# Attention with decay and a softplus MLP: an early load of lam, other PSUM banks for chunk 0's state sums, and a new order of the opening steps

## The chip, the cores and the metric

The kernel runs on one core of one Trainium2 chip. The metric is the device time of one execution in microseconds (us), the median of several runs. An engine works through its own instruction stream in order and waits on semaphores for the others: TensorE (PE) multiplies, VectorE (DVE) and ScalarE (ACT) do elementwise work, SyncE (SP) issues most loads, and GpSimd (POOL) fills a few constants at the start.

## The reference

Two layers follow each other. The first is linear attention with a decay `lam` for each head, computed block by block with a running state; its output, 3072 tokens of 512 features, is the input `x` of an MLP with a softplus between two matrix products.

```python
for b in range(nb):                      # 12 blocks of 64 positions
    intra = einsum(q, k) * Dmask         # Dmask = lam ** (i - j) for i >= j
    intra = einsum(intra, v)
    inter = einsum(q * lam_pow, kv_state)
    out[:, :, sl] = intra + inter
    kv_state = lam_block * kv_state + einsum(k * rev_pow, v)
h = x @ w_in                             # 512 -> 2048
g = log1p(exp(-|h|)) + max(h, 0)         # softplus
return g @ w_out                         # 2048 -> 512
```

## The kernel before

The sequence is cut into 6 chunks of 128 positions, and the 8 heads into 4 pairs; a chunk and a pair make a unit, so that units 0 to 3 are chunk 0 and unit 4 is the first of chunk 1. The batch of 4 lies inside a unit. In chunk 0 the state is zero, so the first products are whole 128 x 128 score blocks (`scores0`, step S), masked on DVE (`mask0_scores`, m), multiplied with v (`out0`, O) and copied out as a high and a low half (`x0_high` on ACT, xh, and `x0_low` on DVE, xl). The state that chunk 1 starts from is the product of the decayed k with v (`k0_decay` or `k0_decay_act`, then `sums0`, Q), which ACT copies out of PSUM (`states0`, sc).

The MLP has 16 slices of d_ff for each chunk, 96 "slots" in all: slot s multiplies x with a slice of `w_in` (`mlp1`, step mlp; 12 products of 128 x 512), ACT and DVE make the softplus and its high and low halves (act, ghi, glo), and `mlp2` multiplies them with a slice of `w_out` (12 products). Each operand is a high and a low half, so every product is taken three times. The weights come as 64-bit floats and are converted on the chip once, in 32 half-megabyte pieces: scale and round and the high half (hi) on ACT; shift, sign, add and the low half (lo) on DVE. Piece numbers stand behind the step names: `lo 8 9` is the low half of pieces 8 and 9, and `mlp 0 2` is slot 0 with pair 2. Piece 8 is needed by `mlp2` of slot 2.

The order of the work is written out by hand. A string of some 170 steps is carried out first, in one order for all engines: each step appends its instructions to the streams of the engines it uses. Then a loop over slots 6 to 99 follows. Loads are steps as well (qk, v, kt for a unit's parts, load n for weight pieces up to n, unit n for whole units) and go to SP's queue; before the first scores a short second string gives the first loads. `warm n` issues n products on zeros, whose result is not used.

The eight PSUM banks form three pools: four "o" banks (`obank`: the zero products, chunk 0's scores, slots 2 and 3, then the four output sums of `mlp2`), one "t" buffer of two banks (`work`: z of chunk 0, the state sums y0, then scores and outputs of the later units, one after the other), and two "h" banks for the other slots' `mlp1`. A tile takes a buffer of its pool when an earlier tile there has been read for the last time.

Constants come from `lam_b`, lam spread over 128 partitions: a copy and a scan on DVE give the mask of chunk 0 (`mask0`), a copy on ACT and a second scan on DVE the powers `lp`.

Of the kernel before, what the change touches and what calls it, by code (L numbers as in the profile page):

```python
# [14 lines left out]
B, H, S, D = 4, 8, 768, 64  # L15
# [11 lines left out]
def half(i):  # L27
    return slice(i * 64, (i + 1) * 64)
# [3 lines left out]
def decay_attention_softplus_ffn(  # L32
# [7 lines left out]
    nc = tc.nc  # L40
# [7 lines left out]
    def t8(shape, dt, name):  # L48
        return sb.tile(shape, dt, tag="b8", bufs=21, name=name)
# [10 lines left out]
    def th(shape, dt, name):  # L60
        return sb.tile(shape, dt, tag="bh", bufs=5, name=name)

    def obank(name):
        return ps.tile([128, 512], F32, tag="o", bufs=4, name=name)

    def work(name):

        return ps.tile([128, 2, 512], F32, tag="t", bufs=1, name=name)
# [4 lines left out]


    lam_b = cp.tile([128, H], F32, name="lam_b")

    def load_lam():
        nc.scalar.dma_start(out=lam_b, in_=lam.rearrange("(o h) -> o h", o=1).broadcast_to([128, H]))

    units, raws = {}, {}  # L80

# [5 lines left out]
    def load_half(g, major):  # L87
        nc.sync.dma_start(out=unit(g)[:, major], in_=att[g // NP, g % NP, :, major])
# [18 lines left out]
    def kt_of(g):  # L107
        return part(g, 1, 0)

    def vt_of(g):  # L110
        return part(g, 1, 1)
# [10 lines left out]
    def w_load(n):  # L122
# [9 lines left out]
            n_raw += 1  # L132

    load_half(0, 0)
    load_lam()
    loads = {
        "qk": lambda g: load_half(g, 0), "v": lambda g: load_part(g, 1), "kt": lambda g: load_part(g, 0),
        "w": w_load, "unit": load_upto,
    }
    for line in "w 1".split(","):  # L140
        name, number = line.split()
        loads[name](int(number))

# [2 lines left out]
    warm = t8([128, 512], F32R, "warm")  # L146
# [3 lines left out]
    def keep_warm(n):  # L150
        for _ in range(n):
            nc.tensor.matmul(warm_ps, lhsT=warm[:, :128], rhs=warm, start=True, stop=True)

    keep_warm(18)

    mask0, step0 = (spare[:, 2 * n : 2 * n + 2].rearrange("q n (h i) -> q (n h) i", i=C) for n in range(2))
    begin0 = begin[:, 0:2].rearrange("q n (h i) -> q (n h) i", i=C)
# [16 lines left out]
        out=begin0, in_=ramp.rearrange("q (o i) -> q o i", o=1).broadcast_to([128, H, C]), scalar=0.0,  # L174
# [81 lines left out]
    lo, hi = half(0), half(1)  # L256
# [149 lines left out]
    x0, z, y = {}, {}, {}  # L406
# [42 lines left out]

    def sums0(*pairs):  # L450
        for p in pairs:
            if not y:
                y[0] = work("y0")
            kd, v = kt_of(p), vt_of(p)
            for b in range(B):
                for t in range(2):
                    c = (p % 2) * 256 + b * D
                    nc.tensor.matmul(
                        y[0][half(t), p // 2, c : c + D], lhsT=kd[:, b, t], rhs=v[:, b, t], start=True, stop=True
                    )  # L460

    def states0(p):
        st = states[p + NP] = th([128, B, 2, D], F32, f"st_{p + NP}")
        for t in range(2):
            c = (p % 2) * 256
            nc.scalar.copy(  # L466
                out=st[lo, :, t], in_=y[0][half(t), p // 2, c : c + 256].rearrange("q (b e) -> q b e", b=B)
            )

    def scores1(g):  # L470
# [3 lines left out]
    def out1(g):  # L474
# [3 lines left out]
    step = {  # L478
        "S": scores0, "m": mask0_scores, "O": out0, "xh": x0_high, "xl": x0_low, "kd": k0_decay, "kda": k0_decay_act,
        "Q": sums0, "sc": states0, "kd1": k_decay, "qd": q_decay, "sc1": scores1,  # L480
        "m1": lambda g: mask_scores(g, z[g][:, 0]), "up": lambda g: update_states(g, z[g][:, 1]), "out1": out1,
        "xh1": lambda g: x_high(g, z[g]), "xl1": lambda g: x_low(g, z[g]),
# [3 lines left out]
        "warm": keep_warm, "load": w_load, "unit": load_upto, "qk": loads["qk"], "v": loads["v"], "kt": loads["kt"],  # L486
    }
    for line in """
        round 0, qk 1, S 0, m 0 0, load 2, scale 0, m 0 1, shift 0, sign 0, scale 1, v 0, qk 2, warm 6, S 1,
        add 0, load 3, m 1 1, warm 2, O 0, m 1 0, hi 0, xh 0, shift 1, lo 0, sign 1, S 2, scale 2, xl 0, v  # L490
        1, qk 3, m 2 0, warm 2, mlp 0 0, v 2, load 4, m 2 1, O 1, round 2, round 1, shift 2, xh 1, kt 1, S
        3, add 1, sign 2, hi 1, scale 3, xl 1, kda 1, lo 1, O 2, mlp 0 1, round 3, xh 2, mlp 1 0, v 3, m 3
        1, load 5, m 3 0, mlp 1 1, add 2, kt 2, load 6, scale 4, shift 3, hi 2, xl 2, O 3, sign 3, lo 2, mlp
        0 2, kda 2, load 7, load 8, add 3, xh 3, kt 0, round 4, hi 3, unit 5, xl 3, shift 4, lo 3, mlp 1 2,
        scale 5, mlp 2 0, shift 5, mlp 0 3, scale 6 7, kt 3, sign 4, load 9, mlp 2 1, mlp 2 2, round 6 7,
        mlp 3 0, mlp 1 3, mlp 3 1, kda 0, shift 6 7, add 4, act 0, kd1 4, load 10, sign 6 7, ghi 0, sign 5,
        add 6 7, hi 4, hi 6 7, kd 3, glo 0, mlp 3 2, lo 6 7, load 11, lo 4, load 12, round 5, mlp 3 3, act
        1, mlp 2 3, Q 0, ghi 1, add 5, Q 1, scale 8 9, load 13, glo 1, hi 5, Q 2, shift 8 9, lo 5, Q 3, sc
        0, sign 8 9, act 2, load 14, sc 3, sc 1, sc 2, sc1 4, load 15, up 4, ghi 2, round 8 9, glo 2, act 3,
        mlp 5, m1 4, mlp 4, ghi 3, unit 6, unit 7, add 8 9, scale 10 11, hi 8 9, qd 4, mlp2 0, round 10 11,  # L500
        glo 3, act 4, shift 10 11, lo 8 9, sign 10 11, ghi 4, glo 4, add 10 11, load 16, mlp2 1
    """.replace("\n", " ").split(","):
        name, *numbers = line.split()
        step[name](*map(int, numbers))
# [7 lines left out]
    for s in range(6, last + LAG):  # L512
# [25 lines left out]
        if s in outs_at:  # L538
            g = outs_at[s]
            w = work(f"z{g}")  # L540
# [46 lines left out]
```

## Time and profile before

| what | value |
|---|---|
| median of 3 runs | 612.82 us (612.53 to 613.39) |
| the profiled execution | 613.22 us, its span 611.4 us |
| PE busy | 598.3 us, 98% of the span |
| DVE, ACT busy | 226.3 us, 211.2 us |
| moved by DMA | 48.95 MB, 20.00 MB of it in the first 60 us |

Times in the profile count from the start of the span. A row of the timeline shows start, length, engine, line and operation, output and input tiles, and a count; the bracket at its end is the idle time before it and what ended it. A row of the windows shows each engine's busy time and instructions in one stretch, then the granted TensorE clock, the DMA engines' busy share and the GB/s.

### The profile page before, as it was taken

To read this page: it belongs to the slowest core of one execution; us is meant where nothing else is said; L and a number is where in the kernel's file an instruction comes from. 1 tells how busy PE (TensorE), PEld (TensorE's weight loads), DVE (VectorE), ACT (ScalarE), POOL (GpSimd) and SP (SyncE) were. 2 spreads that over 40 slices of the span, in tenths; PEclk is the share of its full clock that TensorE was granted. 3 is DMA by queue.
4 is the path that set the end of the run, shared out by engine and by line. 5 is a ranking of instruction groups with operands and counts; after the bars stand their busy time and mean duration, and the time that the engine had idled before them with its cause. 6 is when DMAs were issued, how large, how long until landed. Compare 5 with 4: busy or idle time off the path is not lost.

```text
span 611.4 us, 11189 instructions
## 1 busy us (share of the span) xinstructions
PE 598.3 (98%) x5020; PEld 488.2 (80%) x5020; DVE 226.3 (37%) x337; ACT 211.2 (35%) x343; POOL 1.5 (0%) x9
## 2 busy tenths in 40 slices
PE   7969999999999999999999999999999999999997
PEld 5758888888888888888888888888888888888886
DVE  5978799833321232322313322222222121210111
ACT  3877677633222222321232232212322221322121
POOL 0000000000000000000000000000000000000000
PEclk9979999999999999999999999999999999999999
DMA  8994314205002024201020500210500100100001
GB/s 294 416 417 187 133 70 138 70 2 207 2 2 70 1 70 140 68 1 46 26 70 33 175 2 1 70 42 29 207 1 1 70 1 1 70 0 1 1 1 69
DMA packets 15743, 48.95 MB, mean 80 GB/s; under 512 B 1872, under 2 KB 1872, under 8 KB 15696
## 3 DMA queue, kind: packets, MB, share of 16 engines
q1 hardware_dynamic: 15264, 47.72, 21.3%
q8 instruction: 39, 0.64, 0.4%
q10 hardware_dynamic: 432, 0.53, 0.2%
q14 instruction: 8, 0.07, 0.0%
HBM read 41.95 MB, written 6.29 MB: 79 GB/s over the span
## 4 chain that ended last, share of the span: by engine, by line
PE 93%; DVE 3%; ACT 1%; issue 1%; DMA 1%; DVEq 0%
PE h L363 43%; PE o L380 43%; PE w L285 3%; PE z L298 2%; PE z L302 2%; DMA lam_b<-in_lam 1%; PE w L287 1%; DVE c L225 1%; DVE att L419 1%; ACT st L466 0%; DVE c L231 0%; ACT w L234 0%; PE z L429 0%; DVE c L221 0%; ACT l L344 0%
## 5 line engine op out<-in xcount | busy, mean ns | idle before, releaser
L363 PE MATMUL h<-x,w 128*128 128x512 f32 x1152 | 283.8, 396 | 0.4 <-DVE x L439 0.4
L380 PE MATMUL o<-w,g 128*128 128x512 f32 x1152 | 275.9, 389 | 0.0
L380 PEld LDWEIGHTS o<-w,g 128*128 128x128 f32 x1152 | 216.3, 188 | 44.8
L363 PEld LDWEIGHTS h<-x,w 128*128 128x128 f32 x1152 | 214.2, 189 | 47.1 <-DVE x L439 0.9
L352 DVE TENSOR_TENSOR g<-l,g 128x512 fp32r<-128x512 f32 x96 | 66.4, 691 | 264.6 <-ACT g L348 264.4
L344 ACT ACTIVATE l<-h 128x512 f32<-128x512 f32 x96 | 57.1, 595 | 269.7 <-PE h L363 261.5
L348 ACT CAST g<-l 128x512 fp32r<-128x512 f32 x96 | 59.6, 621 | 3.0
L269 ACT ACTIVATE kd<-att,rp 128x256 f32<-128x256 f32 x40 | 18.1, 501 | 59.9 <-DMA att<-in_att 59.9
L312 DVE SCALAR_TENSOR_TENSOR st<-st,lam_c,w 64x256 f32<-64x256 f32 x72 | 31.6, 479 | 4.3 <-PE w L287 3.5
L285 PEld LDWEIGHTS w<-att 64*64 64x64 f32 x640 | 21.1, 139 | 11.8 <-issue 6.0
L285 PE MATMUL w<-att 64*64 64x64 f32 x640 | 23.9, 226 | 5.0 <-ACT st L466 5.0
L335 DVE TENSOR_TENSOR x<-z,x 128x512 fp32r<-128x512 f32 x20 | 13.8, 691 | 35.2 <-ACT x L328 35.2
L274 DVE TENSOR_TENSOR qd<-att,lp 128x512 f32<-128x512 f32 x20 | 13.8, 689 | 34.1 <-DMA att<-in_att 34.1
L328 ACT CAST x<-z 128x512 fp32r<-128x512 f32 x20 | 11.7, 585 | 38.9 <-PE z L302 38.9
L287 PE MATMUL w<-att,kd 64*64 64x64 f32 x576 | 23.9, 227 | 0.0
L307 DVE TENSOR_TENSOR a<-w,mask 128x512 f32<-128x512 f32 x20 | 13.8, 690 | 25.7 <-PE w L287 19.5
L298 PEld LDWEIGHTS z<-qd,st 64*64 64x64 f32 x640 | 17.0, 134 | 7.0 <-issue 7.0
L287 PEld LDWEIGHTS w<-att,kd 64*64 64x64 f32 x576 | 21.1, 139 | 0.0
L298 PE MATMUL z<-qd,st 64*64 64x64 f32 x640 | 20.9, 224 | 0.0
L231 DVE CUSTOM_DVE_ANT_0 c<-raw,c 128x2048 uint16<-128x2048 uint16 (+1 forms) x19 | 20.0, 1054 | 1.4
L238 DVE TENSOR_TENSOR w<-c,w 128x1024 fp32r<-128x1024 f32 (+1 forms) x19 | 19.9, 1053 | 1.6 <-ACT w L234 1.3
L225 DVE SCALAR_TENSOR_TENSOR c<-raw,c 128x1024 uint32<-128x1024 uint32 (+1 forms) x19 | 19.9, 1054 | 0.4
(42 smaller groups left out, 183.2 us busy)
## 6 DMA issues: line engine op xcount, KB each, us to landing
att<-in_att SPq DMA_DIRECT2D x44, 512.0 KB, 4.8
raw<-in_wts SPq DMA_DIRECT2D x32, 512.0 KB, 8.7
out_dram<-ob SPq DMA_DIRECT2D x22, 256.0 KB, 2.4
att<-in_att SPq DMA_DIRECT2D x8, 256.0 KB, 7.8
out_dram<-ob ACTq DMA_DIRECT2D x2, 256.0 KB, 2.0
lam_b<-in_lam ACTq DMA_DIRECT2D x1, 4.0 KB, 6.4
```

Of the source, the lines that this page charges most:

```text
L225: nc.vector.scalar_tensor_tensor(out=c, in0=raw_at(ks, 1), scalar=0x80000000, in1=c, op0=ALU.bitwise_and, op1=ALU.bitwise_or)
L231: nc.vector.tensor_add(out=c, in0=c, in1=raw_at(ks, 0))
L238: nc.vector.tensor_sub(out=w[:, 1], in0=conv.pop(ks[0]).bitcast(F32), in1=w[:, 0])
L285: nc.tensor.matmul(x[r, cols], lhsT=k[r, b, t], rhs=q[r, b, t], start=True, stop=True)
L287: nc.tensor.matmul(y[half(1 - s), cols], lhsT=kd[r, b, t], rhs=v[r, b, t], start=True, stop=True)
L298: nc.tensor.matmul(w[half(t), s, cols], lhsT=st[r, b, t], rhs=qd[r, b, t], start=True, stop=False)
L312: nc.vector.scalar_tensor_tensor(out=to[:, :, t], in0=of[:, :, t], scalar=lam_c[r, h : h + 1], in1=u[:, :, t], op0=ALU.mult, op1=ALU.add,)
L344: nc.scalar.activation(l_tiles[s], h_tiles.pop(s), AF.Softplus)
L348: nc.scalar.copy(out=g_tiles[s][:, 0, :], in_=l_tiles[s])
L352: nc.vector.tensor_sub(out=g[:, 1, :], in0=l_tiles.pop(s), in1=g[:, 0, :])
L363: nc.tensor.matmul(h_tiles[s], lhsT=w[:, i, cs], rhs=x[:, j, :], start=p == 0 and n == 0, stop=p == NP - 1 and n == 2,)
L380: nc.tensor.matmul(o_tiles[c][b], lhsT=g[:, i, b * 128 : (b + 1) * 128], rhs=w[:, j], start=f == 0 and n == 0, stop=f == NF - 1 and n == 2,)
```

## The change

1. `load_lam`, a DMA on ACT's queue behind the first load of q and k, is gone; the same DMA is now the first one on SP's queue.
2. `sums0` takes its tiles from the "o" pool, one for pairs 0 and 1 and one for pairs 2 and 3, where one buffer of the "t" pool held all four; `states0` reads there.
3. The string of opening steps up to the loop is new, and nine loads, with a half of unit 2 and 3 among them, stand ahead of the first step where one stood. The zero products number 16 + 6 + 3 where they were 18 + 6 + 2 + 2. The loop from slot 6 on is not touched.

```diff
     lam_b = cp.tile([128, H], F32, name="lam_b")
-
-    def load_lam():
-        nc.scalar.dma_start(out=lam_b, in_=lam.rearrange("(o h) -> o h", o=1).broadcast_to([128, H]))
+    nc.sync.dma_start(out=lam_b, in_=lam.rearrange("(o h) -> o h", o=1).broadcast_to([128, H]))
...
     load_half(0, 0)
-    load_lam()
...
-    for line in "w 1".split(","):
+    for line in "w 1, qk 1, w 2, v 1, v 0, qk 2, w 3, qk 3, kt 2".split(","):
...
-    keep_warm(18)
+    keep_warm(16)
...
     def sums0(*pairs):
         for p in pairs:
-            if not y:
-                y[0] = work("y0")
+            if p % 2 == 0:
+                y[p // 2] = obank(f"y{p}")
...
-                        y[0][half(t), p // 2, c : c + D], lhsT=kd[:, b, t], rhs=v[:, b, t], start=True, stop=True
+                        y[p // 2][half(t), c : c + D], lhsT=kd[:, b, t], rhs=v[:, b, t], start=True, stop=True
...
-                out=st[lo, :, t], in_=y[0][half(t), p // 2, c : c + 256].rearrange("q (b e) -> q b e", b=B)
+                out=st[lo, :, t], in_=y[p // 2][half(t), c : c + 256].rearrange("q (b e) -> q b e", b=B)
...
     for line in """
-        round 0, qk 1, S 0, m 0 0, load 2, scale 0, m 0 1, shift 0, sign 0, scale 1, v 0, qk 2, warm 6, S 1,
...
-        1, mlp 2 3, Q 0, ghi 1, add 5, Q 1, scale 8 9, load 13, glo 1, hi 5, Q 2, shift 8 9, lo 5, Q 3, sc
-        0, sign 8 9, act 2, load 14, sc 3, sc 1, sc 2, sc1 4, load 15, up 4, ghi 2, round 8 9, glo 2, act 3,
...
+        S 0, m 0 0, scale 0, m 0 1, round 0, warm 6, S 1, shift 0, sign 0, add 0, scale 1, m 1 0, m 1 1,
...
+        unit 5, scale 8 9, kd 3, mlp 2 3, add 6 7, ghi 1, mlp 3 3, kd1 4, unit 6, mlp 4, Q 1, Q 2, sc1 4, hi
+        6 7, load 11, Q 3, glo 1, shift 8 9, lo 6 7, qd 4, mlp 5, act 2, sc 1, ghi 2, load 12, sign 8 9, sc
...
```

The lines of the changed kernel are three lower than those of the kernel before. A number behind a tile's name tells tiles of one name apart.

On PE, where the opening ends, this stood before: `y` is the tile of the state sums, `att` a unit's loaded data, `h` a slot's sum, `w` (as an output) the scores of unit 4, whose first two instructions are the last rows.

```order
L363 MATMUL h_330<-x_1_252,w_272 128x512 x6
L363 MATMUL h_309<-x_1_252,w_272 128x512 x3
L458 MATMUL y_378<-att_68 64x64 x8
L458 MATMUL y_378<-att_118 64x64 x8
L458 MATMUL y_378<-att_140 64x64 x8
L458 MATMUL y_378<-att_195 64x64 x8
L285 MATMUL w_438<-att_298 64x64
L287 MATMUL w_438<-att_298,kd_346 64x64
```

Now the sums of pairs 1 and 2 stand there, after slot 4's products:

```order
L360 MATMUL h_388<-x_0_182,w_341 128x512 x6
L360 MATMUL h_388<-x_1_269,w_341 128x512 x6
L455 MATMUL y_271<-att_73 64x64 x8
L455 MATMUL y_409<-att_78 64x64 x8
L282 MATMUL w_418<-att_367 64x64
L284 MATMUL w_418<-att_367,kd_382 64x64
```

Pair 0's sum has moved up, ahead of most of the `mlp1` products, and pair 3's behind unit 4's scores; slot 4 has moved ahead of the scores; the sums are in two tiles.

SP's queue now begins so (`in_wts` are weight pieces; rows with 128x512 are a v or a k part):

```order
L76 DMA lam_b<-in_lam 128x8
L86 DMA att_69<-in_att 128x1024
L127 DMA raw_71<-in_wts 128x1024
L86 DMA att_73<-in_att 128x1024
L127 DMA raw_71<-in_wts 128x1024
L89 DMA att_73<-in_att 128x512
L89 DMA att_69<-in_att 128x512
L86 DMA att_78<-in_att 128x1024
```

The load of lam stands ahead of the first q and k; unit 1's v has moved ahead of unit 0's v and of unit 2.

On DVE these are the rows from the first mask product on (`x_0`, `x_1` as inputs are a pair's two score tiles, `c` a weight piece in work, `x_0_182` the MLP's input):

```order
L416 TENSOR_TENSOR att_69<-x_1_128,spare 128x512
L218 TENSOR_SCALAR c_138<-c_138 128x512
L222 SCALAR_TENSOR_TENSOR c_138<-raw_71,c_138 128x512
L228 ISA c_138<-raw_71,c_138 128x1024
L416 TENSOR_TENSOR att_73<-x_0_148,spare 128x512
L416 TENSOR_TENSOR att_73<-x_1_149,spare 128x512
L218 TENSOR_SCALAR c_161<-c_161 128x512
L235 TENSOR_TENSOR w_178<-c_138,w_178 128x512
L222 SCALAR_TENSOR_TENSOR c_161<-raw_71,c_161 128x512
L436 TENSOR_TENSOR x_0_182<-z_169,x_0_182 128x512
L228 ISA c_161<-raw_71,c_161 128x1024
```

Up to the low half of x (L436 here, L439 before) the order is that of before; behind it the sum of piece 1 (L228) now comes ahead of the next mask products.

More of the change, by code (lines that the diff above doesn't have):

```diff
@@ L488, in decay_attention_softplus_ffn @@
     for line in """
-        round 0, qk 1, S 0, m 0 0, load 2, scale 0, m 0 1, shift 0, sign 0, scale 1, v 0, qk 2, warm 6, S 1,
[L490 to L497, printed above, removed]
-        1, mlp 2 3, Q 0, ghi 1, add 5, Q 1, scale 8 9, load 13, glo 1, hi 5, Q 2, shift 8 9, lo 5, Q 3, sc
@@ L499, in decay_attention_softplus_ffn @@
-        0, sign 8 9, act 2, load 14, sc 3, sc 1, sc 2, sc1 4, load 15, up 4, ghi 2, round 8 9, glo 2, act 3,
-        mlp 5, m1 4, mlp 4, ghi 3, unit 6, unit 7, add 8 9, scale 10 11, hi 8 9, qd 4, mlp2 0, round 10 11,
-        glo 3, act 4, shift 10 11, lo 8 9, sign 10 11, ghi 4, glo 4, add 10 11, load 16, mlp2 1
+        S 0, m 0 0, scale 0, m 0 1, round 0, warm 6, S 1, shift 0, sign 0, add 0, scale 1, m 1 0, m 1 1,
+        shift 1, warm 3, O 0, hi 0, lo 0, round 1, xh 0, sign 1, S 2, xl 0, scale 2, mlp 0 0, add 1, m 2 0,
@@ new lines, in decay_attention_softplus_ffn @@
+        hi 1, O 1, load 4, xh 1, v 2, kt 0, m 2 1, shift 2, round 2, lo 1, xl 1, S 3, v 3, kda 2, mlp 1 0, m
+        3 1, m 3 0, load 5, scale 3, shift 3, kda 0, round 3, mlp 1 1, O 2, O 3, xh 2, Q 0, sign 2, load 6,
+        sign 3, xh 3, mlp 0 1, load 7, add 2, add 3, xl 2, mlp 0 2, xl 3, load 8, scale 4, kt 1, shift 4,
+        scale 5, mlp 1 2, mlp 0 3, shift 5, hi 2, lo 2, hi 3, sign 5, round 5, round 4, mlp 1 3, mlp 2 0,
+        load 9, act 0, scale 6 7, lo 3, sign 4, add 5, ghi 0, add 4, mlp 2 1, kda 1, hi 4, mlp 3 0, hi 5,
@@ new lines, in decay_attention_softplus_ffn @@
+        round 6 7, mlp 3 1, shift 6 7, glo 0, kt 3, mlp 2 2, lo 4, act 1, mlp 3 2, load 10, lo 5, sign 6 7,
+        unit 5, scale 8 9, kd 3, mlp 2 3, add 6 7, ghi 1, mlp 3 3, kd1 4, unit 6, mlp 4, Q 1, Q 2, sc1 4, hi
+        6 7, load 11, Q 3, glo 1, shift 8 9, lo 6 7, qd 4, mlp 5, act 2, sc 1, ghi 2, load 12, sign 8 9, sc
+        0, sc 3, glo 2, sc 2, load 13, load 14, round 8 9, m1 4, act 3, ghi 3, unit 7, mlp2 0, up 4, scale
+        10 11, add 8 9, glo 3, hi 8 9, shift 10 11, mlp2 1, load 15, act 4, lo 8 9, load 16, ghi 4, round 10
@@ L502, in decay_attention_softplus_ffn @@
+        11, sign 10 11, glo 4, add 10 11
     """.replace("\n", " ").split(","):
```

## The prediction

> **What bounds the kernel now.** I read the page first for the engine that is nearly always busy, then the windows for where it is not, then the timeline of PE and of what it waits for.
>
> ```profile
> PE 598.3 (98%) x5020; PEld 488.2 (80%) x5020; DVE 226.3 (37%) x337; ACT 211.2 (35%) x343; POOL 1.5 (0%) x9
> ```
> ```profile
> 1.40:5.20 3.80, 3.75 (x9) 2.98 (x10) 0.74 (x1) 0.61 (x1) 0.73 (x2) 1.00 0.56 123
> 10.00:20.00 10.00, 7.77 (x79) 5.68 (x79) 9.93 (x20) 6.11 (x11) 0.00 (x0) 1.00 1.04 415
> 20.00:36.30 16.30, 15.58 (x155) 12.54 (x153) 16.24 (x26) 15.52 (x29) 0.00 (x0) 1.00 1.03 418
> 36.30:39.30 3.00, 0.03 (x2) 0.00 (x0) 3.00 (x6) 2.95 (x6) 0.00 (x0) 1.00 1.01 410
> 39.30:41.20 1.90, 0.00 (x0) 0.00 (x0) 0.64 (x1) 1.84 (x7) 0.00 (x0) 0.51 1.03 418
> 41.20:46.10 4.90, 4.81 (x71) 4.12 (x72) 2.61 (x6) 1.72 (x4) 0.00 (x0) 0.50 1.02 417
> 50.00:60.00 10.00, 10.00 (x104) 8.18 (x103) 8.90 (x10) 6.91 (x11) 0.00 (x0) 1.00 0.32 119
> 60.00:80.00 20.00, 20.00 (x206) 16.24 (x206) 16.14 (x21) 14.01 (x19) 0.00 (x0) 1.00 0.33 109
> 80.00:100.00 20.00, 20.00 (x206) 16.30 (x205) 19.07 (x23) 14.57 (x19) 0.00 (x0) 1.00 0.29 103
> 100.00:600.00 500.00, 500.00 (x4121) 409.31 (x4121) 140.62 (x219) 140.60 (x237) 0.00 (x0) 1.00 0.14 47
> ```
>
> From 50 us on PE never stops, so whatever the opening saves is saved at the end, as long as DVE, ACT and the loads still keep ahead of an earlier PE. In the opening PE loses time in two ways: it waits, and at 39.30 its granted clock falls to 0.50 and stays there up to about 46.1.
>
> ```profile
> 1.45 6.12 PE L152 MATMUL warm_ps<-warm 128*128 128x512 f32 x18 [1.45 <-DVE warm L147]
> 7.50 1.16 PE L413 MATMUL x<-att 64*128 64x128 f32 x16
> 12.45 1.16 PE L413 MATMUL x<-att 64*128 64x128 f32 x14 [1.78 <-DVE att L419]
> 21.50 1.09 PE L429 MATMUL z<-att 128*64 128x128 f32 x16 [0.72 <-DVE x L439]
> 22.53 2.37 PE L363 MATMUL h<-x,w 128*128 128x512 f32 x9
> 34.25 2.08 PE L458 MATMUL y<-att 128*64 128x64 f32 x64
> 41.29 0.36 PE L285 MATMUL w<-att 64*64 64x64 f32 x1 [4.96 <-ACT st L466]
> 50.15 8.32 PE L380 MATMUL o<-w,g 128*128 128x512 f32 x36
> 58.41 0.34 PE L298 MATMUL z<-qd,st 64*64 64x64 f32 x8
> 65.17 0.27 PE L285 MATMUL w<-att 64*64 64x64 f32 x1
> 66.26 0.97 PE L363 MATMUL h<-x,w 128*128 128x512 f32 x3
> ```
> ```profile
> 36.17 1.14 ACT L213 ACTIVATE c<-raw 128x1024 f32<-128x1024 f32 x1
> 37.71 0.76 ACT L466 COPY st<-y 64x256 f32<-64x256 f32 x2
> 38.50 0.60 ACT L344 ACTIVATE l<-h 128x512 f32<-128x512 f32 x1
> 38.99 2.25 ACT L466 COPY st<-y 64x256 f32<-64x256 f32 x6
> ```
>
> The largest wait is 4.96 us: unit 4's scores need the one "t" buffer, which holds the state sums until ACT, busy throughout, has made eight copies of them (3.0 us with its softplus put aside). The clock drop follows that wait. The waits before it, 1.78 and 0.72 us among them, name DVE. DVE is busy 9.93 of 10 us and 16.24 of 16.30, so up to 36 us it sets the pace, and it started late, since it waited for lam:
>
> ```profile
> 7.22 0.69 DVE L187 COPY spare<-lam_b 128x1016 f32<-128x1016 f32 x1 [5.08 <-DMA lam_b<-in_lam]
> 8.02 2.29 DVE L182 TENSOR_TENSOR_SCAN spare<-spare,begin 128x1024 f32<-128x1024 f32 x1
> 11.70 1.28 DVE L419 TENSOR_TENSOR att<-x,spare 128x512 f32<-128x512 f32 x2
> 14.70 1.28 DVE L419 TENSOR_TENSOR att<-x,spare 128x512 f32<-128x512 f32 x2
> 15.89 0.42 DVE L221 TENSOR_SCALAR c<-c 128x512 uint32<-128x512 uint32 x1
> 16.23 0.69 DVE L238 TENSOR_TENSOR w<-c,w 128x512 fp32r<-128x512 f32 x1
> 16.83 0.68 DVE L225 SCALAR_TENSOR_TENSOR c<-raw,c 128x512 uint32<-128x512 uint32 x1
> 43.42 1.79 DVE L312 SCALAR_TENSOR_TENSOR st<-st,lam_c,w 64x256 f32<-64x256 f32 x4 [3.49 <-PE w L287]
> 49.39 1.22 DVE L238 TENSOR_TENSOR w<-c,w 128x1024 fp32r<-128x1024 f32 x1
> 50.52 1.22 DVE L225 SCALAR_TENSOR_TENSOR c<-raw,c 128x1024 uint32<-128x1024 uint32 x1
> ```
>
> **The change part by part.** I take the first mask product as the zero of the new opening and call its start M; before, M is 11.70.
>
> *Lam first.* The chain from lam to M is fixed work: 11.70 - 7.22 = 4.5 us. When lam lands on SP's queue no row shows; these are the nearest:
>
> ```profile
> lam_b<-in_lam ACTq DMA_DIRECT2D x1, 4.0 KB, 6.4
> out_dram<-ob ACTq DMA_DIRECT2D x2, 256.0 KB, 2.0
> ```
> ```profile
> 5.00:6.00 1.00, 1.00 (x5) 0.85 (x4) 0.00 (x0) 0.00 (x0) 0.00 (x0) 1.00 0.66 181
> 6.00:7.00 1.00, 1.00 (x6) 0.79 (x5) 0.00 (x0) 0.00 (x0) 0.00 (x0) 1.00 1.03 414
> ```
>
> Lam takes 6.4 us to land beside SP's loads, and meanwhile these move at 181 GB/s in the sixth microsecond, against 414 in the seventh, when it is done. I read this as the two queues taking turns, each slowing the other. On one queue the 4 KB of lam are simply ahead. Bounds from an issue at 0.73: landed at 2.7 (as the 2.0 us of a far larger transfer) and at 7.2 (6.4, no better). I take 3.5, nearer the first, as nothing is left to take turns with. Then lam's chain is done at 3.5 + 4.5 = 8.0. Every other load goes out one SP issue later, some 0.4 us; as the first scores need q and k only at 7.0, and they lie behind 4 KB alone, I charge nothing. If the loads instead stay as slow as now, unit 0 lands at 7.5 and the first scores wait 0.4.
>
> The Trainium skill ("DMA: Bandwidth & Descriptors", Queues, rings and completion order) states that a DMA engine takes the queue rows in turn, packet by packet. The slow stretch up to 6 us agrees, and the sum by that rule is the one above.
>
> *Sixteen zero products.* 18 took 7.50 - 1.45 = 6.05 us, nine of them in the first 3.80 (0.42 each), the others at 0.227. Two fewer let the first scores start at 7.05, or, were all 16 at the slow rate, at 1.45 + 16 x 0.42 = 8.2. I take 7.6, the middle, since nothing ties the clock's rise to the kernel. The first scores take 1.16, so M = 7.6 + 1.2 = 8.8, with 8.3 and 9.4 as ends; lam at 8.0 is then not the last. If lam comes no earlier, M is 11.7 as now, or 12.1 when everything moves by one SP issue.
>
> The Trainium skill ("TensorE: Matmul & The Clock Gate", Part 1) has PE at half clock until a free-running window of about 3.4 us was busy, and again after an idle one. Of the rise this trace shows a single phase, so that by the page any start between those two ends is as likely. The page's drop after idleness agrees with the fall behind the wait of 4.96 us.
>
> *DVE from M on.* Steps from the rows: two mask products, shift, sign and add 14.70 - 11.70 = 3.00; two mask products 1.19; a shift 0.34; any other 512-wide operation 0.60. The new order up to `xl 2` is: the 3.00; m 1, shift, lo 0, sign 1 (2.73); xl 0, add 1 (1.20); m 2, shift, lo 1, xl 1 (2.73); m 3, shift 3, two signs, two adds (3.93). So `xl 0` starts at M + 5.7 and ends at M + 6.4; `xl 2` ends at M + 13.6 + 0.7 = M + 14.3. Adding 0.2 for waits on itself (the rows have 11.70 to 14.70 with two such), I take 14.5.
>
> *PE from there.* After `xl 0` PE has a last product (0.23), O 1 (22.53 - 21.50 = 1.03), S 3 (1.1), six products held by lo 1 and xl 1 to about M + 10.3, O 2 and O 3 (2.06), Q 0 (a quarter of the 2.05 us that 64 took: 0.51) and five products: M + 14.0. So it waits about half a microsecond for `xl 2`. From then to the end of `mlp2 1` the order holds 46 products of `mlp1` up to slot 4, 12 of slot 5 and 24 of `mlp2`: 82 x 0.227 = 18.6, three Q at 0.51, and unit 4's scores (66.26 - 65.17 = 1.09 at full clock): 21.2 us. `mlp2 1` ends at M + 35.7. Before, it ends at 50.15 + 24 x (58.41 - 50.15)/36 = 55.66.
>
> *The banks.* The 4.96 us stall and the half clock (half of the 4.9 us from 41.2 to 46.1, 2.4 us) are inside this difference: unit 4's scores no longer wait for the copies, since their "t" buffer is free when `xl 3` has run, at about M + 15, and PE reaches them at M + 26. The copies now lie beside slot 5's products. What they may hold instead is the first `mlp2`, which needs all four "o" banks. ACT goes on at the end of O 2 and O 3, M + 12.7. It has 14 operations of 512 (38.99 - 38.50, 0.5 each), four of 1024 (37.71 - 36.17 less one of 0.5, 1.05 each) and two pairs of k's decay (0.8) up to slot 2's softplus: 12.8, so M + 25.5. That softplus, eight copies, ghi 2, a round of 1.05 and slot 3's softplus come to 5.6: the last bank is free at about M + 31.1. PE starts `mlp2` at M + 35.7 - 24 x 0.227 and wants the fourth bank nine products later, M + 32.3. Cover 1.2 us.
>
> *DVE and loads behind an earlier PE.* After `xl 2`, up to the end of `lo 8 9` DVE has 16 operations of 0.60, two shifts of 0.34, three of 0.60 on 1024 elements, five of 1.13 (50.52 - 49.39), four state updates (1.8) and `lo 8 9` itself, 1.22: 20.8, so M + 13.6 + 0.6 + 20.8 + 0.3 = M + 35.3 (0.3 for waits on ACT and on itself). `mlp2` of slot 2 wants it at M + 35.7. Cover 0.4 us, where before it was 55.66 - 50.61 = 5.0. So the stall's gain is nearly the whole of what DVE's lead could pay for. Behind that a slot costs PE 24 x 0.227 = 5.4 us and 1.1 more with attention in it; DVE in 60 to 80 us was busy 16.14 of 20, so that its lead grows again. Loads: 415 GB/s bring a 512 KB piece every 1.26 us. Up to piece 9 SP's queue has 14 transfers of that size and eight of half of it: 22.7 us from about 2 us on. ACT scales the piece after slot 1's softplus, which PE allows ten products behind `xl 2`, at M + 16.8 = 25.6 and not sooner; nothing is late.
>
> **Sum.** M + 35.7 = 44.5 in place of 55.66: 11.2 us. Covers of 0.4 and 1.2 us over 20 us of dense order may not both hold; I take 0.7 us off, an estimate between nothing and the two together. 613.22 - 10.5 = 602.7. The execution profiled lies 0.4 us over the median of the runs, which I leave inside the range: **602.7 us** for the median after.
>
> **The rivals.**
>
> *Lam hardly earlier, or the loads still slow* (M between 10 and 12.1). For it: lam's rows are small however they are queued. Against: the rate leaps when lam is done. The gain is 55.66 - 47.8 = 7.9 at M = 12.1, less 0.7: 606.0; at M = 10, 604.0.
>
> *DVE takes the place of the bound after slot 5.* For it: cover 0.4 us at `lo 8 9`, and 19.07 of 20 us busy between 80 and 100. Against: it idled 0.07 of 10 and 0.06 of 16.3 us when it set the pace, so its own walk is sure. If its operations come 5% later over those 21 us, 1.0 us of which 0.4 is covered, and again behind unit 4's updates, PE loses 1 to 3 us: 604.2 to 605.9.
>
> *The stall moves to the first `mlp2`*, if the copies come late or the two tiles stand in the way of slots 2 and 3 and the change frees nothing. ACT would have to slip 1.2 us; at worst PE pays the 3.0 us of copies: 605.7.
>
> *Slower: lam's 32-byte rows clog the one queue.* Ahead of all loads, each DMA engine has eight of the 128 rows; if every one is waited out before the next, all loads and M move. Slower than before needs M over 55.66 - 35.7 = 20.0, so lam landed after 15.5, or (15.5 - 2)/8 = 1.7 us a row from 2 us on; at 2.2 us a row M is 24.1 and the time 617.3. Against: in 6.4 us all eight were done beside the loads, 0.8 us at most for each.
>
> **How the numbers follow.** The forecast (M 8.3 to 9.4, covers nearly holding: 601.5 to 604) has 0.66; lam or loads late 0.12; DVE the bound 0.13; the stall at `mlp2` 0.05; clogged 0.03; another 0.01 for a difference within 0.2%, which is about what a measurement can tell from none. So faster 0.96, same 0.01, slower 0.03. Low end: M = 8.3 with no slip is 613.22 - 11.7 = 601.5, and 0.3 for the spread of runs: 601.2. High end: lam no earlier, 606.0.
>
> **What would show it.** The mask product's first row at 8.3 to 9.4 us, and lam_b's row under DMA issues at about 2.8 us to landing. PE's idle before unit 4's scores gone, with the clock at 1.00 from 10 us on. The first `mlp2` near 39 us, `mlp2 1` done at 44 to 46. DVE over 98% busy from M to 44 us. It is wrong if M lies above 10, if PE shows a wait of over 1 us on DVE between 24 and 60 us, if the clock falls again, or if a row of `mlp2` waits for the copies.

## The result and the profile after

The changed kernel takes **603.11 us** (603.01 to 603.31), where the kernel before took 613.11 (612.53 to 614.46) beside it: a ratio of 0.9834, 95% interval 0.9817 to 0.9851. The prediction said 602.7, in a range of 601.2 to 606.0. The profiled execution after took 603.04 us with a span of 601.3, against 611.4 before, so the span is 10.1 us shorter.

The engine row of the page, and the windows of the opening, to be read beside those of before (stretch, its length, busy time of PE, PEld, DVE, ACT and POOL, the granted clock, DMA share and GB/s):

```profile
PE 595.7 (99%) x5017; PEld 486.0 (81%) x5017; DVE 226.3 (38%) x337; ACT 211.4 (35%) x343; POOL 1.5 (0%) x9
```
```profile
10.00:20.00 10.00, 9.73 (x99) 7.08 (x99) 9.82 (x18) 6.52 (x12) 0.00 (x0) 1.00 1.04 415
20.00:30.00 10.00, 9.93 (x81) 8.22 (x78) 9.96 (x19) 9.51 (x19) 0.00 (x0) 1.00 1.03 417
30.00:40.00 10.00, 10.00 (x145) 8.29 (x144) 9.94 (x15) 9.86 (x20) 0.00 (x0) 1.00 1.03 417
40.00:50.00 10.00, 10.00 (x104) 8.17 (x103) 9.97 (x13) 9.82 (x14) 0.00 (x0) 1.00 1.03 417
```

PE is busy for 2.6 us less in all, about what the half clock had cost; the rest of the gain is waiting. PE now misses 0.34 us of the 40 us from 10 to 50. DVE and ACT are both nearly full from 20 on, yet PE waits for neither, and the clock row stays at 1.00: the 4.96 us with PE idle and the stretch at 0.51 and 0.50, which stood between 36 and 46, are gone. The timeline of PE shows it row by row:

```profile
1.45 6.47 PE L149 MATMUL warm_ps<-warm 128*128 128x512 f32 x16 [1.45 <-DVE warm L144]
7.84 1.16 PE L410 MATMUL x<-att 64*128 64x128 f32 x16
...
15.63 0.49 PE L360 MATMUL h<-x,w 128*128 128x512 f32 x1 [0.27 <-DVE x L436]
...
22.13 12.21 PE L360 MATMUL h<-x,w 128*128 128x512 f32 x51
34.27 1.15 PE L455 MATMUL y<-att 128*64 128x64 f32 x32
35.36 0.27 PE L282 MATMUL w<-att 64*64 64x64 f32 x1
...
37.06 3.02 PE L360 MATMUL h<-x,w 128*128 128x512 f32 x12
39.92 8.32 PE L377 MATMUL o<-w,g 128*128 128x512 f32 x36
```

Unit 4's scores (35.36) carry no wait in brackets, where there were 4.96 us, and the first `mlp2` starts at 39.92 instead of 50.15. The row behind it starts at 48.17, so `mlp2 1` ends at 39.92 + 24 x (48.17 - 39.92)/36 = 45.4; reckoned in the same way it was 55.66 before. These 10.2 us are, to 0.1, what the whole span lost: nothing is given back in the 550 us behind. On DVE's timeline and under the DMA issues:

```profile
3.41 0.69 DVE L184 COPY spare<-lam_b 128x1016 f32<-128x1016 f32 x1 [1.27 <-DMA lam_b<-in_lam]
...
7.82 0.17 DVE L192 TENSOR_TENSOR rp<-mask,lam_b 128x8 f32<-128x8 f32 x1
9.05 1.29 DVE L416 TENSOR_TENSOR att<-x,spare 128x512 f32<-128x512 f32 x2 [1.07 <-PE x L410]
...
22.89 1.29 DVE L436 TENSOR_TENSOR x<-z,x 128x512 fp32r<-128x512 f32 x2
...
43.23 1.22 DVE L235 TENSOR_TENSOR w<-c,w 128x1024 fp32r<-128x1024 f32 x1
```
```profile
lam_b<-in_lam SPq DMA_DIRECT2D x1, 4.0 KB, 2.7
```

Lam lands 2.7 us after its issue instead of 6.4, and its chain is done at 7.99. The first mask product, M, stands at 9.05, and its bracket names PE: DVE waited 1.07 us for the first scores, so lam is no longer what is late. And the copies of the state sums, on ACT's timeline:

```profile
35.22 0.74 ACT L463 COPY st<-y 64x256 f32<-64x256 f32 x2
...
36.50 2.29 ACT L463 COPY st<-y 64x256 f32<-64x256 f32 x6
```

They still take 3.0 us, ending at 38.79, but now beside unit 4's scores and slot 5's products instead of ahead of them, and 1.1 us before the first `mlp2`.

### The profile page after: what moved, and what is told of

It reads as the page before. It is cut to its first block, busy times and chain, and to the rows that moved or that the text cites. A ratio compares the mean times of both kernels' runs of the same rounds, so it can differ in the third digit from the quotient of the medians.

```text
span 601.3 us, 11190 instructions
## 1 busy us (share of the span) xinstructions
PE 595.7 (99%) x5017; PEld 486.0 (81%) x5017; DVE 226.3 (38%) x337; ACT 211.4 (35%) x343; POOL 1.5 (0%) x9
## 4 chain that ended last, share of the span: by engine, by line
PE 98%; DVE 1%; issue 0%; ACT 0%; DVEq 0%
PE h L360 45%; PE o L377 43%; PE w L282 3%; PE z L295 2%; PE z L299 2%; PE warm_ps L149 1%; PE w L284 1%; PE z L426 0%; PE x L410 0%; PE y L455 0%; DVE att L416 0%; DVE x L436 0%; DVE c L222 0%; ACT x L432 0%; DVE c L218 0%
## 5 line engine op out<-in xcount | busy, mean ns | idle before, releaser
L228 DVE CUSTOM_DVE_ANT_0 c<-raw,c 128x2048 uint16<-128x2048 uint16 (+1 forms) x19 | 19.9, 1056 | 1.5
```

The costliest lines, as they stand in the source:

```text
L228: nc.vector.tensor_add(out=c, in0=c, in1=raw_at(ks, 0))
```

## The experiments

Each run had the kernel before beside it, with medians of 612.67 to 613.40 us. The changed kernel's 603.11 was measured apart from them, so that differences of half a microsecond and less against it are not resolved.

**The parts one at a time.** Lam's load alone, put in the kernel before:

```diff
-    def load_lam():
-        nc.scalar.dma_start(out=lam_b, in_=lam.rearrange("(o h) -> o h", o=1).broadcast_to([128, H]))
+    nc.sync.dma_start(out=lam_b, in_=lam.rearrange("(o h) -> o h", o=1).broadcast_to([128, H]))
...
     load_half(0, 0)
-    load_lam()
```

> The kernel before with the load of lam first on SP's queue and nothing else. Theory A (two separate losses, a late start of DVE and the wait for the one 't' buffer, each worth its own time): the first mask product M moves from 11.7 to about 9.5 (18 zero products, then 1.2 us of scores), everything DVE paces moves with it, the wait of 5 us and the half clock stay: 2.2 us less, 610.9; up to 4 us if the chain of DVE work also loses a wait or two. Theory B (the new order is what buys the time, lam and the banks only matter inside it): no change, 613.

Measured 611.07 (610.05 to 611.68) against 612.91: ratio 0.9966 (0.9957 to 0.9976), 1.84 us. M moved from 11.70 to 9.77. The stall and the half clock stayed, as its PE timeline and windows show:

```profile
1.45 7.18 PE L149 MATMUL warm_ps<-warm 128*128 128x512 f32 x18 [1.45 <-DVE warm L144]
39.34 0.36 PE L282 MATMUL w<-att 64*64 64x64 f32 x1 [4.95 <-ACT st L463]
```
```profile
38.00:45.20 7.20, 5.86 (x74) 4.93 (x75) 3.66 (x7) 3.96 (x9) 0.00 (x0) 0.53 1.03 419
```

So lam first moves the opening by its own gain, and the stall stays as long as it was.

The banks alone, in the kernel before:

```diff
-            if not y:
-                y[0] = work("y0")
+            if p % 2 == 0:
+                y[p // 2] = obank(f"y{p}")
...
-                        y[0][half(t), p // 2, c : c + D], lhsT=kd[:, b, t], rhs=v[:, b, t], start=True, stop=True
+                        y[p // 2][half(t), c : c + D], lhsT=kd[:, b, t], rhs=v[:, b, t], start=True, stop=True
```

> The kernel before with the state sums in two tiles of the 'o' pool and nothing else; old order, lam on ACT's queue. Theory A: the wait of 4.96 us before unit 4's scores and the half clock behind it (2.4 us) go: 7.4 us less, 605.7. Theory B (DVE or the first second-layer products take the place of the wait in the old order, since nothing else was moved): half of it or less, 609 or more, with a new wait of PE on DVE or ACT between 36 and 56 us.

Measured 605.95 (605.88 to 606.05), ratio 0.989 (0.9876 to 0.9905): 6.96 us, with M still at 11.54. Its windows have no idle stretch and no half clock:

```profile
30.00:40.00 10.00, 10.00 (x159) 8.41 (x158) 9.97 (x14) 9.81 (x20) 0.00 (x0) 1.00 1.03 416
40.00:50.00 10.00, 10.00 (x45) 8.28 (x45) 9.77 (x14) 9.79 (x17) 0.00 (x0) 1.00 1.00 406
```

The wait of 4.96 and the 2.4 us charged to the half clock make 7.4, and 6.96 came back; in the profiled executions the first `mlp2` starts 7.37 us earlier (42.78 for 50.15). This is the larger part of the change.

Both edits together, with the old order and its 18 zero products:

> The kernel before with lam first on SP's queue and the state sums in the 'o' pool, in the old order with the old zero products. Theory A: the two add, 2.2 to 4 and 7.4: 602 to 604, that is nearly all of the change, and the order and the loads are worth 0 to 1 us. Theory B: at least 3 us of the change's 10 are missing, 606 or more.

Measured 603.46 (603.03 to 603.95), ratio 0.985 (0.9835 to 0.9865), with M at 9.63. The two edits give 9.45 of the 10 us; for the new order with its two fewer zero products at the start some 0.35 us are left, within the spread of these runs.

The other way about, lam back on ACT's queue in the changed kernel (the first diff reversed):

> The changed kernel with lam back on ACT's queue behind the first q and k. Theory A: M goes from 9.05 back to about 11.7, and the end moves with it less the wait of some 0.3 to 0.5 us that PE has on DVE later: 2.2 to 2.6 us more than the changed kernel, 605.3 to 605.7. Rival (lam is not what sets M; the first scores or the loads are): no difference, 603.1.

Measured 605.78 (605.58 to 605.98): 2.67 us slower than the changed kernel, with M at 11.57, 2.52 later. The end follows M about one to one.

The changed kernel with the sums back in the one "t" buffer. For that the order has to give way, since unit 4's scores could not get the buffer ahead of pair 3's sums:

```diff
-            if p % 2 == 0:
-                y[p // 2] = obank(f"y{p}")
+            if not y:
+                y[0] = work("y0")
...
-        unit 5, scale 8 9, kd 3, mlp 2 3, add 6 7, ghi 1, mlp 3 3, kd1 4, unit 6, mlp 4, Q 1, Q 2, sc1 4, hi
-        6 7, load 11, Q 3, glo 1, shift 8 9, lo 6 7, qd 4, mlp 5, act 2, sc 1, ghi 2, load 12, sign 8 9, sc
-        0, sc 3, glo 2, sc 2, load 13, load 14, round 8 9, m1 4, act 3, ghi 3, unit 7, mlp2 0, up 4, scale
+        unit 5, scale 8 9, kd 3, mlp 2 3, add 6 7, ghi 1, mlp 3 3, kd1 4, unit 6, mlp 4, Q 1, Q 2, Q 3, hi
+        6 7, load 11, glo 1, shift 8 9, lo 6 7, qd 4, act 2, sc 1, ghi 2, load 12, sign 8 9, sc
+        0, sc 3, glo 2, sc 2, sc1 4, mlp 5, load 13, load 14, round 8 9, m1 4, act 3, ghi 3, unit 7, mlp2 0, up 4, scale
```

> The changed kernel with the state sums back in the one 't' buffer; so that the buffer can be passed on, pair 3's sum stands ahead of unit 4's scores, and these behind the four copies, with slot 5 behind them. Theory A (the bank is what holds PE): PE waits for the copies again, and at pair 0's sum for the last low half of chunk 0; by the changed kernel's rows the copies end at about 39 us and PE is there at 35 to 36, so 3 to 4 us, some 1 to 2.5 us at pair 0's sum, and the half clock if a whole idle stretch of over 3.4 us comes of it: 608 to 611. Rival (the new order alone hides the copies): within 1 us of the changed kernel.

Measured 613.04 (610.68 to 614.86), ratio 0.9993 (0.9979 to 1.0006): no gain is left, although M was early (8.09). Two PE waits, and the windows in which they lie:

```profile
24.25 0.69 PE L455 MATMUL y<-att 128*64 128x64 f32 x16 [2.69 <-DVE x L436]
43.54 0.36 PE L282 MATMUL w<-att 64*64 64x64 f32 x1 [3.67 <-ACT st L463]
```
```profile
20.00:30.00 10.00, 7.16 (x53) 5.61 (x50) 7.53 (x14) 6.10 (x12) 0.00 (x0) 0.83 1.03 418
40.00:50.00 10.00, 6.46 (x77) 5.44 (x78) 6.21 (x11) 7.29 (x14) 0.00 (x0) 0.66 1.00 404
```

I had expected one wait and 608 to 611; there are two, and the clock falls after each. The new order asks for pair 0's sums early (`Q 0` ahead of `xl 2`), and with one buffer these wait until DVE has emptied it. So the new order depends on the banks: it can't be credited apart from them.

**What the stall itself costs.** In the kernel before, 20 products into an unread "o" bank just ahead of unit 4's scores. They use up the wait, and only the clock can gain:

```diff
+    def fill(n):
+        f = obank("fill")
+        x = x_of(0, 0)[:, 0]
+        for _ in range(n):
+            nc.tensor.matmul(f, lhsT=x[:, :128], rhs=x, start=True, stop=True)
...
-        1, mlp 2 3, Q 0, ghi 1, add 5, Q 1, scale 8 9, load 13, glo 1, hi 5, Q 2, shift 8 9, lo 5, Q 3, sc
+        1, mlp 2 3, Q 0, ghi 1, add 5, Q 1, scale 8 9, load 13, glo 1, hi 5, Q 2, shift 8 9, lo 5, Q 3, fill 20, sc
```

> The kernel before with 20 products of x with itself, into an 'o' bank that nothing reads, behind the state sums, where PE waits; nothing is left out. They take 20 x 0.227 = 4.5 us of a wait of 5 us. Theory A (the wait costs twice: its length, and the clock that falls behind it): the wait stays and the clock does not fall, 2.0 to 2.4 us less than before, 610.6 to 611. Rival (the clock's fall is no cost of the wait, or costs nothing): 613.

Measured 611.02 (610.93 to 611.08) against 613.40: 2.4 us, ratio 0.9964 (0.995 to 0.9978). The window over the old stall and the scores' row:

```profile
36.30:46.10 9.80, 9.59 (x103) 7.74 (x101) 7.05 (x13) 7.31 (x15) 0.00 (x0) 1.00 1.02 416
```
```profile
41.33 0.27 PE L285 MATMUL w<-att 64*64 64x64 f32 x1 [0.21 <-ACT st L472]
```

The scores start at 41.33, as before (41.29), while the clock stays at 1.00. So the half clock has a price of its own, beside the length of the wait. The medians put it at the 2.4 us that the prediction charged; in the two profiled executions the first `mlp2` starts 2.1 us earlier (48.01 for 50.15). It also varies from execution to execution: in the runs of the kernel before, those with a mean granted clock of 0.997 took 612.39 to 612.74 us, those with 0.992 to 0.994 took 612.70 to 613.84.

**Does the end follow M?** The zero products, 16 in the changed kernel, set to 24, and to 13 in another kernel:

```diff
-    keep_warm(16)
+    keep_warm(24)
```

> The changed kernel with 24 zero products at the start where it has 16. They are ahead of the first scores. Theory A (with lam early, the end of the zero products sets M, and M sets the end): 8 x 0.227 = 1.8 us later, 604.9. Rival (lam's chain or the first load still sets M, or what follows has slack): under 0.5 us.

> The changed kernel with 13 zero products at the start where it has 16. Unit 0's q and k land at 6.7 us there and lam's chain ends at 8.0, so M can be as early as 8.0. If the zero products still set M: 13 at the slow rate end at 1.45 + 13 x 0.42 = 6.9, the scores start 0.9 us earlier than 7.84, M is 8.2 and the time 602.2. Rival: the clock has not risen by then (it rose at 4.6 to 7.5 us in the profiles so far) and the scores themselves run slow; up to half of the gain is lost, 602.6 to 603.

With 24: 604.16 (603.70 to 604.71), 1.05 us slower. In the profiled execution the first scores stand 1.23 us later and the span is 1.2 longer, so the end does follow. The size I had expected for eight products, 1.8, was missed, since the clock rose earlier in this execution than in that of the changed kernel: by the rates of 0.42 and 0.227 a product, the 7.62 us from the first zero product to the first scores make some 11 of 24 products at 0.42 here, and 6.39 us make some 14 of 16 there.

```profile
1.45 7.69 PE L149 MATMUL warm_ps<-warm 128*128 128x512 f32 x24 [1.45 <-DVE warm L144]
9.07 1.16 PE L410 MATMUL x<-att 64*128 64x128 f32 x16
```

With 13: 602.69 (602.48 to 603.17), ratio 0.9838 (0.9824 to 0.9851). This is the lowest time of all, 0.4 us below the changed kernel, but by the ratio to the kernel before it is no gain (0.9838 and 0.9834). M is at 8.07, 1.0 earlier, right behind lam's chain, and the 602.2 that I expected of it did not come. The time of the rival did, though not by its cause: the first scores run at full speed (1.16), and PE waits for loads:

```profile
6.86 1.16 PE L410 MATMUL x<-att 64*128 64x128 f32 x16 [0.32 <-DMA att<-in_att]
...
11.89 1.09 PE L426 MATMUL z<-att 128*64 128x128 f32 x16 [0.30 <-DMA att<-in_att]
13.28 1.16 PE L410 MATMUL x<-att 64*128 64x128 f32 x16 [0.30 <-DMA att<-in_att]
...
20.49 1.09 PE L426 MATMUL z<-att 128*64 128x128 f32 x16 [0.43 <-DMA att<-in_att]
```

By the sums of pairs 1 and 2 only 0.15 us of the lead is left (34.12 for 34.27). The loads are the next bound: an M earlier than 9.05 is no longer worth its whole length.

The same 13 products with both edits in the old order, to weigh the order by itself:

> The old order with lam first, the sums in the 'o' pool and 13 zero products where it has 18: lam_and_banks with the start alone made earlier. If the order is worth nothing: the same as the changed kernel with 13 zero products, within 0.3 us (602 to 602.6). If the new order is worth something of its own where the start is early, since DVE then has to follow: 0.5 us or more over it.

Measured 603.15 (602.75 to 603.66), 0.46 us above the new order on the same chip. The ranges overlap, so the new order is worth some 0.4 us, and this is hardly more than the spread. What it removes can be seen: these waits on DVE, of 0.72 and 0.67 us. The new order has waits for loads of 0.30 and 0.43 in their place (above).

```profile
17.90 1.09 PE L426 MATMUL z<-att 128*64 128x128 f32 x16 [0.72 <-DVE x L436]
21.93 1.09 PE L426 MATMUL z<-att 128*64 128x128 f32 x16 [0.67 <-DVE x L436]
```

**How thin is DVE's cover?** Three more DVE operations of 0.60 us behind `xl 3` (a maximum of the mask with itself, which changes nothing):

```diff
+    def more_dve(n):
+        for _ in range(n):
+            nc.vector.tensor_tensor(out=mask, in0=mask, in1=mask, op=ALU.max)
...
-        sign 3, xh 3, mlp 0 1, load 7, add 2, add 3, xl 2, mlp 0 2, xl 3, load 8, scale 4, kt 1, shift 4,
+        sign 3, xh 3, mlp 0 1, load 7, add 2, add 3, xl 2, mlp 0 2, xl 3, more 3, load 8, scale 4, kt 1, shift 4,
```

> The changed kernel with three more operations of 128x512 on DVE, each the maximum of the mask with itself, right behind the last low half of chunk 0: 3 x 0.60 = 1.8 us more for DVE before it converts pieces 2 to 9. The prediction's cover for DVE (0.4 us, at the low half of pieces 8 and 9): 1.8 - 0.4 = 1.4 us more, 604.5, with PE waits on DVE in slots 2 to 5. Rival (PE is the bound there with slack to spare): no difference, 603.1.

Measured 604.36 (603.88 to 604.60), 1.25 us over the changed kernel. The three operations took longer than planned: they start at 23.89 and the next one at 25.95, so 2.05 us instead of 1.8. In the profiled execution M is 0.20 earlier than in the changed kernel's (8.85) and the first `mlp2` 1.24 later (41.16), so that 1.44 of the 2.05 come through. The cover is some 0.6 us, where the prediction had 0.4. The place is another one, however:

```profile
27.35 8.23 PE L360 MATMUL h<-x,w 128*128 128x512 f32 x35 [1.11 <-DVE w L235]
```

PE waits for the low half of a first-layer piece of slot 2, in the middle of `mlp1`, and at no later place. The thin cover is that of `lo 2`, some 18 us ahead of `lo 8 9`, where I had looked for it.

**Lam's rows and the loads.** The load of lam as the third on SP's queue, behind unit 0 and the first weights:

```diff
-    nc.sync.dma_start(out=lam_b, in_=lam.rearrange("(o h) -> o h", o=1).broadcast_to([128, H]))
...
         loads[name](int(number))
+        if line == "w 1":
+            nc.sync.dma_start(out=lam_b, in_=lam.rearrange("(o h) -> o h", o=1).broadcast_to([128, H]))
```

> The changed kernel with the load of lam third on SP's queue, behind unit 0's q and k and the first weight piece. If lam's 32-byte rows are what holds the loads back at the start, unit 0's q and k, with nothing ahead of them and no second queue, land well before 6.7 us, at 4 to 5, and the loads move over 350 GB/s by the fourth microsecond. Rival: the loads start slowly whatever stands beside them; q and k land at 6.2 to 6.7, less the 0.4 us of one issue. lam lands behind the first piece, at about 8, so M is some 3 us late and the time 606.

It took 606.61 (one run), with M at 12.35 and a PE wait of 2.27. Lam's row under the DMA issues, and the windows microsecond by microsecond:

```profile
lam_b<-in_lam SPq DMA_DIRECT2D x1, 4.0 KB, 6.2
```
```profile
2.00:3.00 1.00, 1.00 (x4) 0.77 (x3) 0.14 (x1) 0.01 (x1) 0.19 (x1) 1.00 1.08 274
3.00:4.00 1.00, 1.00 (x4) 0.81 (x3) 0.00 (x0) 0.00 (x0) 0.00 (x0) 1.00 0.82 180
4.00:5.00 1.00, 1.00 (x3) 0.75 (x3) 0.00 (x0) 0.00 (x0) 0.00 (x0) 1.00 0.93 340
5.00:6.00 1.00, 1.00 (x4) 0.79 (x3) 0.00 (x0) 0.00 (x0) 0.00 (x0) 1.00 0.53 206
6.00:7.00 1.00, 1.00 (x5) 0.82 (x4) 0.00 (x0) 0.00 (x0) 0.00 (x0) 1.00 0.12 35
```

The loads run ahead of those with lam first until lam's rows come, and then the queue moves 35 GB/s. Unit 0's q and k, now first, landed 4.5 us after their issue, at 5.2, a little behind the 4 to 5 that I had expected; the 350 GB/s by the fourth microsecond did not come. To see what these rows cost in all, the last kernel leaves the load out (the decay is then a constant, another computation, and only times are of use), with 13 zero products:

```diff
-    nc.sync.dma_start(out=lam_b, in_=lam.rearrange("(o h) -> o h", o=1).broadcast_to([128, H]))
+    nc.vector.memset(lam_b, 0.98)
```

> Leaves the load of lam out: lam_b is set to 0.98 by a memset on DVE, so the decay is another one and the output is not the reference's. All else as the run with 13 zero products (602.69 us; loads at 48, 164, 229, 303 and 332 GB/s in the five stretches from 2 to 7 us, 1.08 MB in all; first scores at 6.86, 0.32 of it a wait for unit 0's load). Theory: lam's 128 rows of 32 bytes cost the loads 1 to 2 us wherever they stand. Then the loads run near 410 GB/s from the fourth microsecond, at least 1.4 MB by 7 us, unit 0's wait and the two of 0.30 behind it are gone, first scores at 6.5, and the time is 602.0 to 602.3. Rival: the loads climb to their rate by themselves in the first 5 us. Then the five rates stay within 15%, the 0.32 stays and the time is 602.6 to 602.9.

One row of the windows for each kernel, the whole stretch from 2 to 7 us. Before:

```profile
2.00:7.00 5.00, 5.00 (x17) 3.95 (x16) 0.14 (x1) 0.01 (x1) 0.19 (x1) 1.00 0.71 201
```

The changed kernel, lam first:

```profile
2.00:7.00 5.00, 5.00 (x13) 3.90 (x12) 3.62 (x4) 1.08 (x3) 0.19 (x1) 1.00 0.87 211
```

Lam third on the same queue:

```profile
2.00:7.00 5.00, 5.00 (x14) 3.94 (x13) 0.14 (x1) 0.01 (x1) 0.19 (x1) 1.00 0.70 207
```

Thirteen zero products, lam first:

```profile
2.00:7.00 5.00, 4.68 (x15) 3.35 (x15) 3.63 (x4) 1.09 (x3) 0.19 (x1) 1.00 0.86 215
```

And without the load of lam:

```profile
2.00:7.00 5.00, 5.00 (x17) 3.64 (x17) 4.51 (x7) 2.17 (x5) 0.19 (x1) 1.00 0.94 300
```

On a second queue, ahead of the loads or among them, lam leaves them 201 to 215 GB/s; without it they have 300. Against the same kernel with the load, 215 GB/s, the 4 KB cost 5 us x 85 GB/s = 0.43 MB of other transfers, one microsecond at their later 415 GB/s, and about as much in the other two places. The first load alone does feel the place: unit 0's q and k landed 6.3 us after their issue before, with lam on the second queue, 5.6 in the changed kernel, behind lam, and 4.5 and 4.6 with lam third and without it. The rival, that the loads climb by themselves, holds in part: even without lam they are at 221 to 340 from 3 to 6 us and not near 410.

The time did not follow. It is 603.09 (602.45 to 603.51), no faster than with the load, where I had expected 602.0 to 602.3. The first scores stand at 6.75 without a wait for a load, but the lead of the loads is given back between 10 and 14 us (over 2 to 14 us the rate is 335 GB/s without lam and 329 with it), and one load is waited for 0.99 us:

```profile
10.00:11.00 1.00, 1.00 (x14) 0.83 (x11) 0.85 (x2) 0.00 (x0) 0.00 (x0) 1.00 1.02 291
11.00:12.00 1.00, 1.00 (x13) 0.64 (x13) 1.00 (x3) 0.82 (x2) 0.00 (x0) 1.00 0.99 328
12.00:13.00 1.00, 0.51 (x10) 0.27 (x6) 1.00 (x3) 0.84 (x2) 0.00 (x0) 1.00 0.92 336
13.00:14.00 1.00, 0.50 (x8) 0.53 (x10) 1.00 (x3) 0.14 (x1) 0.00 (x0) 1.00 0.97 377
```
```profile
13.50 1.16 PE L410 MATMUL x<-att 64*128 64x128 f32 x16 [0.99 <-DMA att<-in_att]
```

There the transfer engines are busy at 0.92 to 1.02 and move 291 to 377 GB/s, where the same stretch with lam has 401 to 442. Why they slow there stays open.

## Why the prediction was right, point by point

The time was 0.4 us off, and the mechanism and most of the terms were as forecast. That it came so close is in part luck: M was 0.25 us late and PE's path from there 0.65 longer, and the 0.7 taken off for covers that in fact held made up for most of this.

- **What bounds it.** Right: what the opening saves is saved at the end (10.2 us at `mlp2 1`, 10.1 of span).
- **Lam.** Taken as landed at 3.5; it is 0.73 + 2.7 = 3.4, and its chain ends at 7.99 where 8.0 was forecast. Right, and being ahead is what does it: third on the same queue, lam took 6.2 us.
- **Sixteen zero products.** First scores at 7.84 for 7.6, M at 9.05 for 8.8, inside the ends 8.3 and 9.4. Fewer products were fast than in the profile before: by the two rates, 0.42 and 0.227, some 14 of the 16 were slow, where of the 18 before some 10 were. (Nine products at 0.42 and nine at 0.227, as in the sum, make 5.8 us, while the 18 took 6.05; its window ended at 5.20, before the rise.)
- **DVE from M on.** `xl 2` ends at 22.89 + 0.69 = 23.58, M + 14.5. To the tenth.
- **PE from there.** `mlp2 1` done at M + 36.4, not 35.7. The 0.7 taken off for thin covers happens to be this size, but it is not what was lost: both covers held. `lo 8 9` ends at 44.45 and is wanted at 45.4, the copies end at 38.79, and no row waits for either. What was lost lies in the spacing of the products. From the end of `xl 2` to the sums of pairs 1 and 2 PE has 46 products in 34.27 - 23.58 = 10.69 us, 0.232 each; the twelve of slot 5 take (39.92 - 37.06)/12 = 0.238 each and the 24 of `mlp2` 0.229, where the sum has 0.227 for all 82. That is 0.4 us, and the three sums, 1.70 us for 1.53, are another 0.2. The rows of before had the spacing already: 0.229 in `mlp2` ((58.41 - 50.15)/36) and 0.233 in the 36 `mlp1` products ahead of the sums ((34.25 - 25.86)/36). This term was mis-sized, and a slip booked elsewhere paid for it.
- **The banks.** Right in place and nearly in price: 6.96 us alone for 7.4 (4.96 and 2.4), and the filled wait gives 2.1 to 2.4 by itself.
- **The loads.** Here a step failed: "I read this as the two queues taking turns, each slowing the other." Then, with lam ahead on one queue, nothing should have been left that slows the loads. They stayed slow, 211 GB/s for 201, and 207 with lam in third place, where they have 300 without it. What costs them is the load of lam itself, on one queue as on two. The wait of 0.4 us that I named for this case ("if the loads instead stay as slow as now") did not come all the same: unit 0 landed at 1.16 + 5.6 = 6.8 and not at 7.5, since behind lam it took 0.7 us less than beside it (so much of the reading holds), and the first scores were not ready before 7.84. So this slip cost the forecast no time. With 13 zero products a wait of 0.32 came. The rule of the Trainium skill that the prediction weighed there ("DMA: Bandwidth & Descriptors", Queues, rings and completion order: a DMA engine takes its queue rows in turn) explains neither the 35 GB/s with everything on one queue nor the nearly equal totals. The Specifications of the same page of the Trainium skill name 512 bytes as the least transfer at line rate, and lam's rows of 32 bytes lie far below; the direction agrees, but no price for such rows stands there.
- **DVE's cover.** Size near, some 0.6 for 0.4; place wrong. I followed the piece that looked latest by the sum (`lo 8 9`), which had 1.0 us to spare, and the first to be late is a piece of slot 2, some 18 us earlier.
- **The new order.** I walked through it as it stood and never priced it against the old one. It is worth about 0.4 us, hardly to be told from the spread, and it works only with the banks.
- **Rivals.** None came, though of the first ("or the loads still slow") the condition did, without moving M above 10. The clogged queue, the slower one, is refuted in size and not in kind: the rows do hold up the queue, by about 1 us up to 7 us, while it needed 12: lam landed at 3.4, and slower than before began at 15.5. The range given for DVE as the bound, 604.2 to 605.9, does not follow from its own 1 to 3 us: on top of 602.7 they make 603.7 to 605.7.

## What to carry to other kernels

A wait on the bounding engine may cost more than its length: here 4.96 us of idle PE brought a stretch at half clock that cost another 2.1 to 2.4 us, so look at the granted clock behind every wait of over 2 us, and at buffers that only a busy engine can empty. A tiny broadcast that a long chain hangs on belongs ahead of the large loads, because it cost these about the same up to 7 us in all three places tried, and only the chain can win. After such a gain look for the next late input: here a further 1.0 us off the opening was worth 0.4 at most, because the loads were next.

## What the runs showed of the hardware

**The rise of the clock moves from execution to execution.** The same 18 zero products open the kernel before and the one with lam alone, but they took 6.12 us in the one and 7.18 in the other. By the two rates some 10 were slow in the one and some 16 in the other. With lam early this is 1.1 us of M that no edit made. (The slow products are known by their length alone: the granted clock of the windows reads 1.00 there too.) The Trainium skill ("TensorE: Matmul & The Clock Gate", Part 1) says that the window is free-running and that the number of slow products varies from run to run; these rows agree. An edit of half a microsecond in the opening can't be judged by one profile.

**The clock fell after waits of 2.69 and 2.27 us.** The first is in the kernel with one buffer (0.83 over 20 to 30 us, above), the second in the one with lam third, whose PE rows and window are these:

```profile
13.09 1.90 PE L411 MATMUL x<-att 64*128 64x128 f32 x14 [2.27 <-DVE att L417]
14.92 1.65 PE L150 MATMUL warm_ps<-warm 128*128 128x512 f32 x3
```
```profile
10.00:20.00 10.00, 7.73 (x64) 5.54 (x64) 9.73 (x18) 5.71 (x10) 0.00 (x0) 0.83 1.04 416
```

Three zero products take 1.65 us there, 0.97 in the changed kernel. The same part of the Trainium skill speaks of an idle window of about 3.4 us; here 2.3 us of waiting were enough, while the wait of 1.78 in the kernel before left the clock at 1.00. What else in the stretch counts as idle no run here shows.

**A load of 4 KB in 32-byte rows cost the other loads about a microsecond up to 7 us**, in each of the three places tried, on two queues, as shown above. By 14 us the difference is down to 0.07 MB. Whether the shortness of the rows, their number or the spreading of one row over 128 partitions costs this, no run here separates.
